# Up projections by Strassen's scheme in an attention kernel with two feed-forward layers

## The chip, the core and the metric

The kernel runs on one core of one Trainium2 chip. The metric is the device time of one execution in microseconds (us). The engines are TensorE (PE for its matmuls, PEld for its weight loads), VectorE (DVE), ScalarE (ACT), GpSimd (POOL) and SyncE (SP), which here issues nearly all DMAs.

## The reference

```python
B, H, S, D = 4, 8, 576, 64           # masked softmax attention, 32-wide local or strided masks
attn = softmax(mask(q @ k.T / sqrt(D))) @ v
x = attn.transpose(0, 2, 1, 3).reshape(2304, 512)
h = x @ w_in                          # 512 -> 2048
x = (h * tanh(log(1 + exp(h)))) @ w_out            # 2048 -> 512
h = maximum(maximum(x @ w1, x @ w2), x @ w3)       # three up projections, 512 -> 768
out = h @ w_out2                      # down projection, 768 -> 512
```

Inputs are drawn at random; the weights come to the chip as 8-byte floats and are taken apart there.

## The kernel before

Every fp32 product is made of three matmuls: each operand is kept as a high and a low part (fp32r), and `PASSES` names the pairs high·high, high·low, low·high. So one 128-feature by 512-token block with its four slices of 128 input channels takes 12 matmuls. Tokens lie in five blocks, four of 512 and one of 256.

The stages overlap only at their ends. Attention; then `raw`, the first four of sixteen feature blocks of `w_in`; then their part of `w_out` into x2, stored to DRAM (`x2p`); then the other twelve feature blocks (`into_h`, L516, and x2 matmuls L543, called the h stage here), block of tokens by block of tokens, with the stored part added (`whole`, L563 to L570) and x2 split into high and low parts; then the last layer, called the up stage here: for each block of tokens and each of six feature blocks three up projections (`up`, L590) into a ring of four PSUM banks, the maximum of the three (`m1` on ACT, L596; `m2` on DVE, L599), its split into the high and low halves of `g` (L601, L602), and the down projection (`down`, L615) into `acc0` to `acc3`.

A weight block of 128 x 512 is loaded (L787, L790) into a slot, turned into fp32 by one ACT operation (L253) and three DVE operations (L257, L261, L267), and split by one of ACT (L277) and one of DVE (L281). There are 24 slots. The weights of the last layer are converted while the h stage ends, in its last block of 256 tokens.

The order on each engine is not that of the code: `build_plan` adds every step with its engine, estimated cost, and what it reads and writes to a `Plan`; the plan simulates the engines, gives each step a due time by running backward, repeats this, and writes out the best order. The engines work through their lists in that fixed order, and wait for each other by semaphores. Where the plan sees PE idle before the first x2 matmul, it puts matmuls on zeros (`fill`).

Of the kernel before, what the change touches and what calls it, by code (L numbers as in the profile page):

```python
# [10 lines left out]
F32 = mybir.dt.float32  # L11
F32R = mybir.dt.float32r
# [15 lines left out]
SLOTS_Y = 8  # L28
W_EXP = 8
EB = 96  # L30
REST = 5376
# [158 lines left out]
def build_plan(k, B, H, S, D, DM, FF, FF2, wide):  # L190
# [33 lines left out]
    for f in range(F1, FC):  # L224
        for kind in ("in", "out"):
            order.append((kind, f))
            need[kind, f] = n_a1 + f - F1
    for f in range(F2C):
        for j, kind in enumerate(("1", "2", "3", "out2")):
            order.append((kind, f))  # L230
            need[kind, f] = n_a + 1.5 * f + 0.3 * j
    slot_of = {}
    free_slots = [("a", i) for i in range(SLOTS_A)]

    def load_and_convert(key):
# [8 lines left out]
        extra = {"x": [("attn",)], "y": [("hrdone",)]}.get(slot[0], [])  # L244
# [5 lines left out]
        add("w_load", "sp", nbytes / 360, load, reads=extra, writes=[hk, lk] if wide else [wk], rank=rank - 3)  # L250
        if wide:
# [23 lines left out]

        def hi():
            nc.scalar.copy(out=k.open_slot(slot)[:, 0, :], in_=k.wt(r2).bitcast(F32))  # L277

        def lo():
            s = k.slot(slot)  # L280
            nc.vector.tensor_tensor(out=s[:, 1, :], in0=k.wt(r2).bitcast(F32), in1=s[:, 0, :], op=ALU.subtract)  # L281

        add("w_hi", "act", act(512), hi, reads=[wk], writes=[hk], rank=rank)
        add("w_lo", "dve", dve(512), lo, reads=[wk, hk], writes=[lk], rank=rank)
# [263 lines left out]

    def part(s, bi):
        t0, n = blocks[bi]  # L550
        for c in range(KC):
            e = ring("ev")
            add("ev", "act", act(n, psum=True), (lambda c=c, e=e: nc.scalar.mul(k.work("ev", e)[:, :n], k.bank(f"acc{c}")[:, :n], W_SCALE)),
                reads=[("bank", f"acc{c}")], writes=[("ev", e)], rank=s)
            add("x2p_st", "sp", P * n * 4 / 360, (lambda c=c, e=e: nc.sync.dma_start(out=k.x2p[:, c, t0:t0 + n], in_=k.work("ev", e)[:, :n])),
                reads=[("ev", e)], writes=[("x2p", bi, c)], rank=s)

    def whole(s, bi):
# [19 lines left out]
    def up(bi, f, rank):
        rm, rg = ring("h"), ring("g")
        MK, G0, G1 = ("h", rm), ("g", rg, 0), ("g", rg, 1)  # L580
        t0, n = blocks[bi]
        m_ = lambda: k.work("h", rm)[:, :n]
        g = lambda: k.g(rg)
        for w_ in ("1", "2", "3"):
            hb = hring[hcount[0] % len(hring)]
            hcount[0] += 1
            for c in range(KC):
                def h_mm(c=c, hb=hb, w_=w_):
                    for m, (a, q) in enumerate(PASSES):
                        nc.tensor.matmul(  # L590
                            k.bank(hb)[:, :n], lhsT=wap((w_, f), a, c), rhs=k.x[:, q, c, t0:t0 + n],
                            start=(c == 0 and m == 0), stop=(c == KC - 1 and m == 2),
                        )
                add("u_mm", "pe", 3 * mm(n), h_mm, reads=wkeys((w_, f)) + [("x2", bi, c)], writes=[("bank", hb)], rank=rank)
            if w_ == "1":
                add("m1", "act", act(n, psum=True), (lambda hb=hb: nc.scalar.copy(out=m_(), in_=k.bank(hb)[:, :n])),  # L596
                    reads=[("bank", hb)], writes=[MK], rank=rank)
            else:
                add("m2", "dve", dve(n), (lambda hb=hb: nc.vector.tensor_tensor(out=m_(), in0=k.bank(hb)[:, :n], in1=m_(), op=ALU.max)),  # L599
                    reads=[("bank", hb)], writes=[MK], rank=rank)  # L600
# [6 lines left out]
    def down(bi, f, rg, rank):  # L607
        t0, n = blocks[bi]
        key = ("out2", f)
        for c in range(n // P):  # L610
            ab = f"acc{c}"
# [8 lines left out]
            if f == F2C - 1:  # L620
                o_ = ring("wt")
                o = lambda o_=o_: k.wt(o_).bitcast(F32)
                if c % 2:
                    add("o", "dve", dve(DM), (lambda ab=ab, o=o: nc.vector.tensor_scalar(
                        out=o(), in0=k.bank(ab)[:], scalar1=W_SCALE, scalar2=None, op0=ALU.mult)),
                        reads=[("bank", ab)], writes=[("wt", o_)], rank=rank)
                else:
                    add("o", "act", act(DM, psum=True), (lambda ab=ab, o=o: nc.scalar.mul(o(), k.bank(ab)[:], W_SCALE)),
                        reads=[("bank", ab)], writes=[("wt", o_)], rank=rank)
                add("o_st", "sp", P * DM * 4 / 360, (lambda c=c, o=o: nc.sync.dma_start(  # L630
                    out=k.out[t0 + c * P:t0 + (c + 1) * P, :], in_=o())), reads=[("wt", o_)], rank=rank)
# [5 lines left out]
    free_slots.extend(("x", i) for i in range(SLOTS_X))  # L637
    s = 0
    for bi in range(NB1):
        for f in range(F1):  # L640
            raw(s, bi, f, RAW_BANKS[s % len(RAW_BANKS)])
            s += 1
    for f in range(F1):
        release(("in", f))
# [8 lines left out]
    add("ypool", "dve", 0, k.open_ypool, writes=[("hrdone",)], rank=s - 1)  # L653
    free_slots.extend(("y", i) for i in range(SLOTS_Y))
# [4 lines left out]
    for bi, (t0, n) in enumerate(blocks):  # L659
        for c in range(KC):  # L660
            e = ring("ev")
            xp_ring[bi, c] = e
            add("x2p_ld", "sp", P * n * 4 / 360, (lambda c=c, e=e, t0=t0, n=n: nc.sync.dma_start(
# [227 lines left out]
```

## Time and profile before

| what | value |
|---|---|
| median of 3 runs | 801.85 us (801.34 to 802.04) |
| profiled execution: span from first to last instruction | 801.2 us |
| PE matmul busy | 793.7 us, 99% of the span |
| DVE busy | 361.0 us, 45% |
| ACT busy | 321.1 us, 40% |

The page gives no other time for the profiled execution than its span; the three timed runs lie 0.1 to 0.8 us above it, which is what lies around a span. A PE that reads 99% busy has nearly no gap in front of a matmul; how long one matmul keeps PE is read from the starts of matmuls that follow each other, since the busy time of each overlaps the next.

### The profile page before, as it was taken

The numbers are of one execution on the slowest core, as the hardware profiler recorded it, in microseconds if no ns is written. First come the engines' busy times: TensorE is split into PE (matmuls) and PEld (weight loads), VectorE is DVE, ScalarE is ACT, GpSimd is POOL, SyncE is SP. The second block draws the span as 40 slices with busy tenths as digits, with TensorE's granted clock in tenths as the row PEclk, the third lists the DMA queues.
The fourth block names the chain that finished last, engine by engine and source line by source line (L and its number), as shares of the span: only waits on it lengthen the run. The fifth ranks groups of instructions, "written<-read, shape, count | busy, mean of one in ns | idle before, by whom it ended". The sixth has DMA issues, their size and how long they took to land.

```text
span 801.2 us, 12605 instructions
## 1 busy us (share of the span) xinstructions
PE 793.7 (99%) x5017; PEld 670.4 (84%) x5017; DVE 361.0 (45%) x769; ACT 321.1 (40%) x839; POOL 4.4 (1%) x22
## 2 busy tenths in 40 slices
PE   9999999999999999999999999999999999999998
PEld 7878888988888888888888889888888888888897
DVE  6998886895941311311221169981222221122222
ACT  5988878996731322321322257631110111110111
POOL 2000000000000000000000000000000000000000
PEclk9999999999999999999999999999999999999999
DMA  9787750944900100100010069300100010010010
GB/s 212 156 158 125 134 105 22 351 149 163 334 2 1 53 0 1 54 0 1 1 53 0 1 224 325 109 1 0 53 1 0 13 41 1 0 53 1 0 53 27
DMA packets 119690, 59.66 MB, mean 74 GB/s; under 512 B 91984, under 2 KB 110416, under 8 KB 119632
## 3 DMA queue, kind: packets, MB, share of 16 engines
q1 hardware_dynamic: 118448, 58.57, 26.2%
q8 instruction: 39, 0.64, 0.3%
q10 hardware_dynamic: 1184, 0.30, 0.2%
q14 instruction: 19, 0.16, 0.1%
HBM read 49.41 MB, written 9.44 MB: 73 GB/s over the span
## 4 chain that ended last, share of the span: by engine, by line
PE 88%; DMA 4%; SPq 3%; DVE 3%; ACT 1%; issue 1%; DVEq 0%; ACTq 0%
PE bank_acc L543 23%; PE bank_a L590 21%; PE bank_a L516 12%; PE bank_acc L615 9%; PE bank_h L516 7%; PE bank_h L590 7%; PE bank_acc L516 3%; DMA wslot<-in_moe_w_dram 1%; DMA v<-in_v_dram 1%; PE bank_a L413 1%; PE bank_a L471 1%; SPq L809 1%; PE bank_a L458 1%; PE bank_acc L413 1%; PE bank_acc L471 1%; DMA wslot<-in_moe_w_out_dram 1%
## 5 line engine op out<-in xcount | busy, mean ns | idle before, releaser
L543 PE MATMUL bank_acc<-g,wslot 128*128 128x512 f32 (+1 forms) x960 | 205.1, 369 | 1.5 <-DVE g L538 0.7
L543 PEld LDWEIGHTS bank_acc<-g,wslot 128*128 128x128 f32 x960 | 168.3, 188 | 33.6 <-DVE g L538 2.0
L590 PE MATMUL bank_a<-x,wslot 128*128 128x512 f32 (+1 forms) x816 | 173.2, 367 | 0.0
L590 PEld LDWEIGHTS bank_a<-x,wslot 128*128 128x128 f32 x816 | 142.4, 189 | 25.5
L538 DVE TENSOR_TENSOR g<-h,g 128x512 fp32r<-128x512 f32 (+1 forms) x80 | 50.9, 636 | 192.1 <-ACT g L537 192.0
L516 PE MATMUL bank_a<-x,wslot 128*128 128x512 f32 (+1 forms) x540 | 116.2, 368 | 0.0
L516 PEld LDWEIGHTS bank_a<-x,wslot 128*128 128x128 f32 x540 | 94.6, 189 | 16.8
L599 DVE TENSOR_TENSOR h<-bank_a,h 128x512 f32<-128x512 f32 (+1 forms) x46 | 29.1, 633 | 137.3 <-PE bank_a L590 137.3
L615 PE MATMUL bank_acc<-wslot,g 128*128 128x512 f32 x324 | 78.3, 389 | 0.0
L516 PE MATMUL bank_h<-x,wslot 128*128 128x288 f32 (+2 forms) x372 | 74.2, 338 | 0.0
L615 PEld LDWEIGHTS bank_acc<-wslot,g 128*128 128x128 f32 x324 | 60.4, 188 | 12.3
L535 ACT ACTIVATE h<-bank_a 128x512 f32<-128x512 f32 (+1 forms) x45 | 25.0, 554 | 108.8 <-PE bank_a L516 108.8
L516 PEld LDWEIGHTS bank_h<-x,wslot 128*128 128x128 f32 x372 | 58.5, 188 | 7.1
L601 ACT ACTIVATE g<-h 128x512 fp32r<-128x512 f32 (+1 forms) x30 | 17.6, 588 | 114.9 <-DVE h L599 114.9
L590 PE MATMUL bank_h<-x,wslot 128*128 128x512 f32 (+1 forms) x264 | 58.3, 370 | 0.0
L438 ACT ACTIVATE s<-s,st 118x54 f32<-118x54 f32 (+1 forms) x160 | 55.2, 348 | 7.0 <-DVE st L432 6.7
L590 PEld LDWEIGHTS bank_h<-x,wslot 128*128 128x128 f32 x264 | 46.7, 188 | 8.6
L537 ACT CAST g<-h 128x512 fp32r<-128x512 f32 (+1 forms) x80 | 46.1, 577 | 4.4 <-PE bank_acc L543 2.6
L253 ACT ACTIVATE wt<-wslot 128x512 f32<-128x512 f32 x56 | 37.9, 678 | 21.6 <-DVE wslot L281 9.6
L277 ACT CAST wslot<-wt 128x512 fp32r<-128x512 f32 x56 | 34.3, 620 | 14.7 <-DVE wt L267 14.3
L596 ACT COPY h<-bank_a 128x512 f32<-128x512 f32 (+1 forms) x22 | 12.0, 547 | 69.0 <-PE bank_a L590 69.0
L281 DVE TENSOR_TENSOR wslot<-wt,wslot 128x512 fp32r<-128x512 f32 x56 | 38.2, 684 | 2.6 <-ACT wslot L277 2.5
(71 smaller groups left out, 680.2 us busy)
## 6 DMA issues: line engine op xcount, KB each, us to landing
wslot<-in_moe_w_out_dram SPq DMA_DIRECT2D x22, 512.0 KB
wslot<-in_moe_w_dram SPq DMA_DIRECT2D x18, 512.0 KB
wslot<-in_moe_w_in_dram SPq DMA_DIRECT2D x16, 512.0 KB
out_dram<-wt SPq DMA_DIRECT2D x18, 256.0 KB
x2p<-ev SPq DMA_DIRECT2D x16, 256.0 KB
ev<-x2p SPq DMA_DIRECT2D x16, 256.0 KB
rawq<-in_q_dram SPq DMA_DIRECT2D x48, 72.0 KB
rawk<-in_k_dram SPq DMA_DIRECT2D x48, 72.0 KB
```

The costliest lines, as they stand in the source:

```text
L253: nc.scalar.mul(k.wt(r2).bitcast(F32), k.words(slot)[1].bitcast(F32), 2.0 ** -111)
L277: nc.scalar.copy(out=k.open_slot(slot)[:, 0, :], in_=k.wt(r2).bitcast(F32))
L281: nc.vector.tensor_tensor(out=s[:, 1, :], in0=k.wt(r2).bitcast(F32), in1=s[:, 0, :], op=ALU.subtract)
L438: nc.scalar.activation(sv()[:, j, :], sv()[:, j, :], AF.Exp, bias=mx()[:, j:j + 1], accum_out=dn()[:, j:j + 1],)
L516: nc.tensor.matmul(k.bank(hb)[:, :n], lhsT=wap(("in", f), a, c), rhs=k.x[:, q, c, t0:t0 + n], start=(c == 0 and m == 0), stop=(c == KC - 1 ...
L535: add(name, "act", act(n, psum=not stored), lambda: nc.scalar.activation(Hh(), src(), AF.Mish, scale=W_SCALE), reads=sread, writes=[HK], r ...
L537: add("gh", "act", act(n), lambda: nc.scalar.copy(out=g()[:, 0, :n], in_=Hh()), reads=[HK], writes=[G0], rank=s)
L538: add("gl", "dve", dve(n), lambda: nc.vector.tensor_tensor(out=g()[:, 1, :n], in0=Hh(), in1=g()[:, 0, :n], op=ALU.subtract), reads=[HK, G0 ...
L543: nc.tensor.matmul(k.bank(f"acc{c}")[:, :n], lhsT=wap(("out", f), a, c), rhs=g()[:, q, :n], start=(first and m == 0), stop=(last and m == 2),)
L590: nc.tensor.matmul(k.bank(hb)[:, :n], lhsT=wap((w_, f), a, c), rhs=k.x[:, q, c, t0:t0 + n], start=(c == 0 and m == 0), stop=(c == KC - 1 a ...
L599: add("m2", "dve", dve(n), (lambda hb=hb: nc.vector.tensor_tensor(out=m_(), in0=k.bank(hb)[:, :n], in1=m_(), op=ALU.max)), reads=[("bank", ...
L615: nc.tensor.matmul(k.bank(ab)[:], lhsT=k.g(rg)[:, a, c * P:(c + 1) * P], rhs=t[:, q, :], start=(f == 0 and m == 0), stop=(f == F2C - 1 and ...
```

## The change

The three up projections are taken out of `up`. Features go in pairs of 128-blocks, tokens in pairs of 384 (`SP`), so x2 falls into three "pairs" of tokens. With the left operand (two feature blocks by two halves of the 512 channels: A11, A12, A21, A22) and the right operand (two halves of the channels by two halves of the tokens: B11 to B22), each 256 x 768 output is formed by Winograd's form of Strassen's scheme: seven products of half blocks (`product`, L722), six matmuls of 384 columns each, where eight would be needed. The outer loop runs over nine sets (three pairs of feature blocks times `w1`, `w2`, `w3`), the inner one over the three pairs of tokens: 27 units.

- Sums of weights S1 to S4 are made when a set's two weights are converted (`set_convert`, four DVE additions of 256 columns), and then split like weights.
- Differences of tokens T1, T2, T3 and N21 are made once per pair (`pair_operands`): 20 DVE operations and 8 low halves on DVE, 8 high halves on ACT, all of 384 columns. N21 takes the place of B12 in `x`. Those of pairs 0 and 1 come in the h stage; pair 2 ends with the last block of tokens, so its own come after it.
- The sums of products are formed in three PSUM banks per unit (two sets of banks take turns). Bank `Bk` is the narrow one: ACT copies the first product into it, three products accumulate onto it, and between these ACT copies it out (`copy(Bk, u2)`) and DVE reads it (`result(Bk, m22, p7)`). A unit with `w1` has two DVE operations and five ACT copies; one with `w2` or `w3` has six DVE operations and three ACT copies.
- The maxima live in the tiles `g`, `h` and `ev`, go to DRAM (`h2`) after the third weight, and come back for the down projection, which is now a stage of its own after all up projections (`h2_ld`, split, `down`), with two sets of four banks in turn.
- There are 16 slots for 24. The twelve feature blocks of the h stage are done in two sweeps of six over all tokens, with the partial x2 stored and loaded once more.

```diff
-SLOTS_Y = 8
+SWEEP = 6
+SP = 384
+T_SLOTS = (5, 6, 7, 8, 9, 10)
+CP_SLOT = 4
...
+    sweeps = [range(f, f + SWEEP) for f in range(F1, FC, SWEEP)]
...
+    def pair_operands(s, p):
...
+            steps = [(lambda: o(a, 0), bt, ALU.subtract, opkeys(p, a, j) + b_key), (t, lambda: o(a, 1), ALU.add, opkeys(p, a, j))]
+            if not b_f32:
+                steps.append((t, lambda: o(b, 1), ALU.subtract, opkeys(p, b, j)))
...
+        for j in range(2):
+            home.clear()
+            difference("T1", "B12", "B11", j)
+            difference("T3", "B22", "B12", j)
+            split("T3", j)
+            difference("T2", "B22", "T1", j)
+            split("T1", j)
+            difference("N21", "B21", "T2", j)
+            split("T2", j)
+            split("N21", j)
...
+    def set_convert(i, rank):
...
+        for out, a, b, op in (
+            ((s12, 0), (w2_, 0), (w2_, 1), ALU.add), ((s12, 1), (s12, 0), (w1_, 0), ALU.subtract),
+            ((s34, 0), (w1_, 0), (w2_, 0), ALU.subtract), ((s34, 1), (w1_, 1), (s12, 1), ALU.subtract),
+        ):
...
+    def strassen(i, w_, f, p, rank):
...
+        A, D, Bk = (("a0", "a2", "acc0"), ("a1", "h0", "acc1"))[u % 2]
+        p7, u2 = ("cp", u % 2), ("h", 2)
...
+                for j in range(2):
+                    for (pa, pb) in PASSES:
+                        nc.tensor.matmul(
+                            k.bank(bank)[:, :SP], lhsT=left(i, a, pa, j), rhs=operand(p, "B12" if b == "N21" else b, pb, j),
+                            start=start and n == 0, stop=n == 5, skip_group_check=True,
+                        )
...
+        product(A, "A11", "B11", True)
+        copy(A, ("bank", Bk))
+        product(D, "S3", "T3", True)
+        copy(D, p7)
+        product(A, "A12", "B21", False)
+        result(A, m11)
+        product(Bk, "S2", "T2", False)
+        copy(Bk, u2)
+        product(D, "A22", "N21", False)
+        result(D, m21, u2)
+        product(Bk, "S1", "T1", False)
+        result(Bk, m22, p7)
+        product(Bk, "S4", "B22", False)
+        result(Bk, m12)
+        if w_ == "3":
...
+                add("h2_st", "sp", P * SP * 4 / 360, (lambda m=m, ff=ff, t0=t0: nc.sync.dma_start(
+                    out=k.h2[:, ff, t0:t0 + SP], in_=home(m))), reads=[m], writes=[("h2", ff, t0 // SP)], rank=rank)
...
     def up(bi, f, rank):
...
-        for w_ in ("1", "2", "3"):
-            hb = hring[hcount[0] % len(hring)]
...
-                add("u_mm", "pe", 3 * mm(n), h_mm, reads=wkeys((w_, f)) + [("x2", bi, c)], writes=[("bank", hb)], rank=rank)
...
+        add("h2_ld", "sp", P * n * 4 / 360, lambda: nc.sync.dma_start(out=m_(), in_=k.h2[:, f, t0:t0 + n]),
+            reads=[("h2", f, b) for b in range(NT // SP) if b * SP < t0 + n and (b + 1) * SP > t0], writes=[MK], rank=rank - 3)
...
+    for w, sweep in enumerate(sweeps):
+        final = w == len(sweeps) - 1
+        for bi, (t0, n) in enumerate(blocks):
+            part_load(w, s, bi)
+            for f in sweep:
...
+            add_part(w, s - 1, bi, final)
...
+            while final and 2 * SP * (pairs_done + 1) <= t0 + n:
+                pair_operands(s, pairs_done)
+                pairs_done += 1
+    u = 0
+    for i, (w_, f) in enumerate(sets):
+        for p in range(n_pairs):
+            strassen(i, w_, f, p, s_end + span * u)
+            u += 1
...
     for bi in range(NB):
         for f in range(F2C):
-            rank = s + 2.0 * (bi * F2C + f)
+            rank = s + 0.5 * (bi * F2C + f)
             ent = up(bi, f, rank)
-            down(*ent, rank + 3)
+            down(*ent, rank + 1)
```

PE in the middle of the last layer, before: in `bank_a0` to `bank_h0` the up projections of one block, in `bank_acc0` to `bank_acc3` the down projection; `x` holds x2.

```order
L590 MATMUL bank_a2_103<-x_66,wslot_4786 128x512 x12
L590 MATMUL bank_h0_104<-x_66,wslot_4806 128x512 x12
L615 MATMUL bank_acc0_105<-wslot_4827,g1_81 128x512 x3
L615 MATMUL bank_acc1_106<-wslot_4827,g1_81 128x512 x3
L615 MATMUL bank_acc2_107<-wslot_4827,g1_81 128x512 x3
L615 MATMUL bank_acc3_108<-wslot_4827,g1_81 128x512 x3
L590 MATMUL bank_a0_101<-x_66,wslot_4844 128x512 x12
L590 MATMUL bank_a1_102<-x_66,wslot_4868 128x512 x12
L590 MATMUL bank_a2_103<-x_66,wslot_4889 128x512 x12
```

PE now, in a unit of the fifth set (`w2`); `ty` holds the T operands of pairs 0 and 1, and bank `acc0` is this unit's `Bk`; a semaphore that the instruction waits for stands in brackets.

```order
L722 MATMUL bank_acc0_110<-ty_2738,wslot_5439 128x384 x6
L722 MATMUL bank_a2_108<-x_66,wslot_5427 128x384 [waits Activation_49]
L722 MATMUL bank_a2_108<-x_66,wslot_5427 128x384 x5
L722 MATMUL bank_acc0_110<-ty_2738,wslot_5439 128x384 [waits Activation_49]
L722 MATMUL bank_acc0_110<-ty_2738,wslot_5439 128x384 x5
L722 MATMUL bank_a1_107<-x_66,wslot_5305 128x384 x6
L722 MATMUL bank_acc0_110<-x_66,wslot_5449 128x384 [waits DVE_49]
L722 MATMUL bank_acc0_110<-x_66,wslot_5449 128x384 x5
L722 MATMUL bank_h0_109<-ty_2738,wslot_5449 128x384 x6
L722 MATMUL bank_acc1_111<-ty_2738,wslot_5439 128x384 [waits Activation_49]
```

Twelve matmuls into one bank became six; the second and third accumulation into `acc0` each wait for ACT or DVE, with one product of another bank in front of them.

DVE in the same stage before: the maxima (L599) and the low half of `g` (L602).

```order
L599 TENSOR_TENSOR h0_73<-bank_h0_104,h0_73 128x512
L599 TENSOR_TENSOR h0_73<-bank_a0_101,h0_73 128x512
L602 SCALAR_TENSOR_TENSOR g0_80<-h0_73,g0_80 128x512
L599 TENSOR_TENSOR h1_74<-bank_a2_103,h1_74 128x512
L599 TENSOR_TENSOR h1_74<-bank_h0_104,h1_74 128x512
L602 SCALAR_TENSOR_TENSOR g1_81<-h1_74,g1_81 128x512
L599 TENSOR_TENSOR h2_75<-bank_a1_102,h2_75 128x512
L599 TENSOR_TENSOR h2_75<-bank_a2_103,h2_75 128x512
```

DVE now, at the start of the Strassen stage: operands of pair 2 (L630 differences in `wt`, L641 low halves) with the first results (L745) among them.

```order
L630 TENSOR_TENSOR wt1_70<-x_66 128x384
L641 TENSOR_TENSOR wslot_4839<-wt2_71,wslot_4839 128x384
L630 TENSOR_TENSOR wt1_70<-wt1_70,x_66 128x384
L630 TENSOR_TENSOR wt0_69<-wt0_69,x_66 128x384
L630 TENSOR_TENSOR wt1_70<-wt1_70,x_66 128x384
L630 TENSOR_TENSOR wt3_72<-wt3_72,x_66 128x384
L630 TENSOR_TENSOR wt0_69<-wt0_69,x_66 128x384
L745 TENSOR_TENSOR g_4833<-bank_a2_108,h2_75 128x384
L641 TENSOR_TENSOR wslot_4842<-wt1_70,wslot_4842 128x384
L641 TENSOR_TENSOR x_66<-wt3_72,x_66 128x384
L630 TENSOR_TENSOR wt2_71<-x_66,wt0_69 128x384
L745 TENSOR_TENSOR g_4834<-bank_acc0_110,wslot_4836 128x384
```

Between two reads that hand a PSUM bank back to PE there now stand operations on SBUF alone, and later in the stage those of the conversion of weights (L264 to L292, L681).

## Rows read from the trace of the kernel before

**Rows 1.** the page: busy time by engine, and the granted clock in 40 slices.
```profile
PE 793.7 (99%) x5017; PEld 670.4 (84%) x5017; DVE 361.0 (45%) x769; ACT 321.1 (40%) x839; POOL 4.4 (1%) x22
...
PEclk9999999999999999999999999999999999999999
```

**Rows 2.** windows by stage: busy us of PE, PEld, DVE, ACT, POOL; clock, DMA.
```profile
160.00:180.00 20.00, 20.00 (x89) 16.55 (x89) 20.00 (x37) 19.36 (x37) 0.00 (x0) 1.00 0.42 153
204.00:464.59 260.59, 260.36 (x1147) 215.03 (x1147) 70.98 (x114) 78.56 (x133) 0.00 (x0) 1.00 0.10 34
464.59:502.61 38.02, 36.88 (x292) 35.53 (x291) 33.15 (x67) 25.41 (x53) 0.00 (x0) 1.00 0.93 307
502.61:797.24 294.63, 294.63 (x1403) 248.12 (x1401) 91.14 (x155) 53.60 (x95) 0.00 (x0) 1.00 0.06 20
```

**Rows 3.** the page: groups of the up and down projections, and a weight load.
```profile
L590 PE MATMUL bank_a<-x,wslot 128*128 128x512 f32 (+1 forms) x816 | 173.2, 367 | 0.0
...
L615 PE MATMUL bank_acc<-wslot,g 128*128 128x512 f32 x324 | 78.3, 389 | 0.0
...
L590 PE MATMUL bank_h<-x,wslot 128*128 128x512 f32 (+1 forms) x264 | 58.3, 370 | 0.0
...
L590 PEld LDWEIGHTS bank_a<-x,wslot 128*128 128x128 f32 x816 | 142.4, 189 | 25.5
```

**Rows 4.** the chain that ended last: start, us, engine, tile, line, count.
```profile
741.48 2.72 PE bank_h L590 x12
...
774.72 1.44 PE bank_h L590 x12
```

**Rows 5.** timeline, PE, matmuls of 288 columns: start, us, engine, line, operation, count.
```profile
148.21 1.76 PE L516 MATMUL bank_acc<-x,wslot 128*128 128x288 f32 x12
149.81 1.76 PE L516 MATMUL bank_h<-x,wslot 128*128 128x288 f32 x12
```

**Rows 6.** groups by line and shape: DVE reading PSUM, 512 and 256 columns.
```profile
L599 DVE TENSOR_TENSOR h<-bank_a,h 128x512 f32<-128x512 f32 x36 | 24.9, 690 | 118.4 <-PE bank_a L590 118.4
...
L599 DVE TENSOR_TENSOR h<-bank_a,h 128x256 f32<-128x256 f32 x10 | 4.3, 425 | 18.9 <-PE bank_a L590 18.9
```

**Rows 7.** the same for ACT.
```profile
L596 ACT COPY h<-bank_a 128x512 f32<-128x512 f32 x18 | 10.5, 586 | 60.2 <-PE bank_a L590 60.2
...
L596 ACT COPY h<-bank_a 128x256 f32<-128x256 f32 x4 | 1.5, 372 | 8.9 <-PE bank_a L590 8.9
```

**Rows 8.** timeline, DVE without idle time: operations that follow each other.
```profile
502.26 1.41 DVE L563 SCALAR_TENSOR_TENSOR ev<-bank_acc,ev 128x256 f32<-128x256 f32 x4
...
506.33 0.68 DVE L261 SCALAR_TENSOR_TENSOR wt<-wslot,wt 128x512 uint32<-128x512 uint32 x1
...
506.93 0.42 DVE L257 TENSOR_SCALAR wt<-wt 128x512 uint32<-128x512 uint32 x1
...
507.27 0.68 DVE L281 TENSOR_TENSOR wslot<-wt,wslot 128x512 fp32r<-128x512 f32 x1
```

**Rows 9.** timeline, hand-over between PE and DVE or ACT.
```profile
484.91 0.43 DVE L538 TENSOR_TENSOR g<-h,g 128x256 fp32r<-128x256 f32 x1
...
485.39 0.77 PEld L543 LDWEIGHTS bank_acc<-g,wslot 128*128 128x128 f32 x6 [0.28 <-DVE g L538]
...
512.84 0.61 PE L590 MATMUL bank_a<-x,wslot 128*128 128x512 f32 x2
...
513.04 0.59 ACT L596 COPY h<-bank_h 128x512 f32<-128x512 f32 x1 [0.49 <-PE bank_h L590]
...
572.68 2.88 PE L615 MATMUL bank_acc<-wslot,g 128*128 128x512 f32 x12
572.88 0.69 DVE L599 TENSOR_TENSOR h<-bank_a,h 128x512 f32<-128x512 f32 x1 [1.96 <-PE bank_a L590]
```

**Rows 10.** timeline, PE in the change of stages, with idle time and its releaser.
```profile
475.79 3.02 PE L543 MATMUL bank_acc<-g,wslot 128*128 128x256 f32 x23 [0.49 <-DVE g L538]
```

**Rows 11.** timeline, the last two stores.
```profile
797.41 1.11 SPq L630 DMA_DIRECT2D out_dram<-wt  x2
```

More of the change, by code (lines that the diff above doesn't have):

```diff
@@ L223, in build_plan @@
         need["in", f], need["out", f] = f, n_raw + f
[L224 to L231, printed above, removed]
+    for i, sweep in enumerate(sweeps):
+        for f in sweep:
+            for kind in ("in", "out"):
+                order.append((kind, f))
+                need[kind, f] = n_a1 + i * NB * SWEEP + f - sweep[0]
     slot_of = {}
-    free_slots = [("a", i) for i in range(SLOTS_A)]
+    free_slots = list(range(SLOTS_A))
     def load_and_convert(key):
@@ L565, in whole @@
                 op0=ALU.mult, op1=ALU.add)), reads=[("bank", ab)], writes=[("ev", e)], rank=s)
-        for c in range(KC):
+            if not last:
+                store_part(i + 1, s, bi, c, e)
+        for c in range(KC) if last else ():
             e = xp_ring[bi, c]
             add("x2_hi", "act", act(n), (lambda c=c, e=e: nc.scalar.copy(out=k.x[:, 0, c, t0:t0 + n], in_=k.work("ev", e)[:, :n])),
-                reads=[("ev", e)], writes=[("x2", bi, c)], rank=s + 0.5)
+                reads=[("ev", e)], writes=[("x2", bi, c, 0)], rank=s + 0.5)
@@ new lines, in build_plan, with set_slots, set_load @@
+    set_of = {}
+    def set_slots(n):
+        got = [x for x in free_slots if x not in RESERVED][:n]
+        for x in got:
+            free_slots.remove(x)
+        return got
+    def set_load(i, w_, f, rank):
+        slot, = set_slots(1)
+        n = len(set_of.setdefault(i, []))
+        set_of[i].append(slot)
+        add("w_load", "sp", P * 4096 / 360, lambda: k.load_weight(w_, f + n, k.stage(slot)),
+            reads=[("attn",)], writes=[("slot", slot, 0), ("slot", slot, 1)], rank=rank)
@@ L578, in up @@
     def up(bi, f, rank):
-        rm, rg = ring("h"), ring("g")
-        MK, G0, G1 = ("h", rm), ("g", rg, 0), ("g", rg, 1)
+        rm, rg = ring("wt"), ring("g")
+        MK, G0, G1 = ("wt", rm), ("g", rg, 0), ("g", rg, 1)
         t0, n = blocks[bi]
-        m_ = lambda: k.work("h", rm)[:, :n]
+        m_ = lambda: k.wt(rm)[:, :n].bitcast(F32)
         g = lambda: k.g(rg)
-        for w_ in ("1", "2", "3"):
-            hb = hring[hcount[0] % len(hring)]
[L586 to L593, printed above, removed]
-                add("u_mm", "pe", 3 * mm(n), h_mm, reads=wkeys((w_, f)) + [("x2", bi, c)], writes=[("bank", hb)], rank=rank)
[L595 to L600, printed above, removed]
@@ L642, in build_plan @@
             s += 1
+    convert_ready()
     for f in range(F1):
@@ new lines, in build_plan, with advance @@
+    n_pairs = NT // (2 * SP)
+    n_set = [0, 0]
+    span = 1.35
+    def advance(s0):
+        room = lambda: len([x for x in free_slots if x not in RESERVED])
+        while True:
+            i, c = n_set[0] // 2, n_set[1]
+            if c < n_set[0] // 2 and room() >= 2:
+                set_convert(c, s0 + span * n_pairs * c - 4)
+                n_set[1] += 1
+            elif i < len(sets) and i <= c and room() >= 1:
+                set_load(i, *sets[i], s0 + span * n_pairs * i - 8)
+                n_set[0] += 1
+            else:
+                return
@@ new lines, in build_plan @@
+    u = 0
[3 more added lines that the diff above has]
+            u += 1
+        free_slots.extend(set_of[i])
+        advance(s_end)
+        if n_set[1] == len(sets):
+            order.extend(("out2", f_) for f_ in range(F2C) if ("out2", f_) not in need)
+            for f_ in range(F2C):
+                need["out2", f_] = s_end + span * len(sets) * n_pairs + f_ * 0.5
+            usable = [x for x in free_slots if x not in RESERVED]
+            free_slots[:] = usable
+            convert_ready()
```

214 lines of the change are left out of this document (168 added, 46 removed), and 3 rows, old and new, of the table M_HOME.

## The prediction

> **What bounds the kernel now.** I read the page first: PE is busy 793.7 of 801.2 us, and its clock stands at full speed (2.4 GHz) in all 40 slices [rows 1]. The reader is to see that no other engine can be the bound on average, and that only fewer or shorter matmuls can bring much. Then the windows by stage [rows 2]. The last layer, 502.61 to 797.24, has PE busy without a gap and DVE at 91.14 of 294.63 us, 31%. The h stage, 204 to 464.59, is much the same. Between them lie 38.02 us in which weights of the last layer are converted while PE runs the block of 256 tokens, with DVE at 33.15, 87%.
>
> Third, what one matmul costs, from starts in the chain and the timeline. Twelve matmuls of 512 columns take 2.72 us, 226.7 ns each, and twelve of 256 take 1.44, 120 ns [rows 4]. At 2.4 GHz the columns alone are 213.3 and 106.7 ns, so both leave 13.3 ns. Twelve of 288 columns take 149.81 - 148.21 = 1.60 us, 133.3 ns, again 120 + 13.3 [rows 5]. A matmul of 384 columns is then 160 + 13.3 = 173.3 ns. This is the number on which all rests; no row shows it, but rows on both sides do.
>
> **Up projections.** Before there are 816 + 264 = 1080 of them [rows 3]: 18 blocks of features and weights, each with 48 of 512 and 12 of 256 columns, so 864 x 0.2267 + 216 x 0.120 = 221.8 us. With the 324 of the down projection at 0.2267 (73.4 us) this is 295.2, and the stage lasts 294.63 with three of them done before it: it holds nothing but matmuls. Now there are 27 units of seven products of six matmuls, 1134 x 0.1733 = 196.6 us. Saved: 25.2 us. Two extra matmuls that open banks `acc0` and `acc1` (L752) give back 0.35. A unit is 7.28 us, a product 1.04.
>
> One rule speaks against smaller matmuls. The trace has a weight load at 189 ns on the mean, longer than the 173 of a matmul [rows 3], yet twelve matmuls with twelve loads pass in 1.44 us: loads lie behind matmuls. The Trainium skill (TensorE: Matmul & The Clock Gate, "The mechanism" in Part 3) says that a weight load overlaps a running matmul only where their row groups differ, and here all use the whole array; with its 107 ns for 128 columns ("LDWEIGHTS (loading the stationary operand)") the saving would be (864 x 0.320 + 216 x 0.214) - 1134 x 0.267 = 20 us, as an estimate from these pages. The 13.3 ns left of 120 speak against it.
>
> **The change of stages.** From 464.59 to 502.61 PE has 12 x 24 = 288 matmuls of 256 columns and three of 512 to do, 35.24 us, and takes 38.02: 2.8 us are lost, such as the 0.49 in which x2 waits for a low half behind conversions on DVE [rows 2, 10]. That stretch goes. In its place the first sweep's last block of 256 tokens has the conversions of eight weights and the first set beside it, with DVE about as full, but for half as long: I take 1.5 us (0 to 2.8). The second storing and loading of partial x2 goes through SP, which has nothing else in the h stage, and its four additions per block on DVE lie beside 32.6 us of matmuls; nothing.
>
> **Operands of pair 2.** They can begin only after the last block, and units 0 and 1 with the first product of unit 2 (some 13 us in PE's list) run before PE needs the first of them. DVE operations follow each other at (1.41 - 0.41) / 3 = 0.33 us with 256 columns and 0.60 with 512 [rows 8]; halfway, 0.47, for 384. 28 of these are 13.2 us; eight of 256 columns for x2 go before, 2.7, less the 1.1 us by which the first bank is ready early. PE needs T3 of both channel slices first, 21 operations in: about 12 us. It just fits; I take 0.5 us (0 to 5, if ACT's halves hold DVE up).
>
> **Hand-backs.** This is what the trace before does not have. In each unit ACT must read `Bk` before S1 x T1 adds to it, and DVE before S4 x B22; in PE's list one product, 1.04 us, stands in front of each. ACT and DVE begin 0.20 us after the product ends, and PE's weight load follows 0.05 after they end [rows 9]. A DVE read of 384 columns is halfway between 425 and 690 ns, 0.56; an ACT copy between 372 and 586, 0.48 [rows 6, 7]. So 0.81 and 0.73 of 1.04 us are used: a margin of 0.23 and 0.31, if the engine is free. It need not be. DVE has 126 result operations (9 units with two, 18 with six) x 0.47 = 59 us, seven sets to convert at 2 x (0.34 + 2 x 0.60) + 4 x 0.33 + 3 x 0.60 + 0.33 = 6.6, so 46, six weights of the down projection at 2.14, 13, and pair 2's 13: 131 of 197 us, 67%. An operation of 0.60 that has just begun spends the margin; behind the late read stand all later ones of DVE's list, and PE waits for these too. Bounds: from 160 to 180 us DVE is busy 20.00 of 20.00 and PE loses nothing; in the change of stages at 87% PE loses 2.78 of 38.02, 7.3%, which would be 14.4 of 197 us [rows 2]. I take 3 us, nearer to the lower end, 0.06 us for each of 54 hand-backs: the load is lower than in both, and the plan has put conversions where it expects a gap.
>
> **Down projection alone.** Its 73.4 us stay. Per block and feature block PE needs 2.72 us; ACT's 0.6 and DVE's 0.6 fit. What was in SBUF now comes from DRAM. The last two stores show the price: issued from 797.41 on, both landed by the end of the span at 801.2, under 3.8 us each [rows 11]. A store and a load are then at most 7.6 us, but only pair 2's data are young, and they are used after three blocks, 49 us later; four `wt` buffers cover loads at 2.72 us a step. What can be late is the first `g`, whose buffers still hold results of pair 1 until stored: one unit of cover, 7.28 us. I take 0.5 us (0 to 2). The end is as before: the last bank, a copy, a store.
>
> **Sum.** 801.2 - 25.2 + 0.35 - 2.8 + 1.5 + 0.5 + 3 + 0.5 = 779.05 us of span. The median of the runs is 0.65 above the span of the profiled execution, so 779.7 us.
>
> **Rivals.**
> - Hand-backs cost at the rate of the change of stages: 14.4 in place of 3 gives 791. For it speaks that lists in fixed order lost just so with DVE at 87%; against it DVE's 67%, and that set 0 and 1 are converted before. Chance 0.2 (784.5 to 797).
> - Slower than before: every hand-back finds a conversion of 0.60 and a maximum of 0.47 in front of it, so is late by 1.07 - 0.25 = 0.8 us; 54 of these are 44, and the time is 821. It decides from 0.46 us on the mean, where 54 x 0.46 eats 25. For it: DVE's maxima follow directly on its reads (L745, L748 in its list). Against: PE's list alternates two units, so it has other banks to work on. Chance 0.06.
> - The change doesn't do what it says: matmuls of 384 columns run at the pace of their weight loads, 189 ns [rows 3]. 1134 x 0.189 = 214.3, a saving of 7.5: 797. Against it stand the 120 ns of 256 columns. The skill's rule above would give some 785, and by that row it falls with this rival. Chance 0.05.
> - Nothing is lost anywhere: 801.2 - 25.2 + 0.35 - 2.8 = 773.6 of span, 774.2. Part of my own range, chance of below it 0.04.
>
> **Numbers.** My forecast has 0.65, from 774.2 to 784.5. The range takes in most of the first rival: 774 to 792. Faster by over 0.2% (about what a measurement of this kernel can tell from no change), below 800.2: 0.65 + 0.2 + 0.05 + 0.04 less a little for 797 being near: 0.92. Within 0.2%: 0.02. Slower: 0.06.
>
> **What would show it.** In the changed profile: products of L722 start 1.04 us after each other where nothing waits (else the pace of 384 columns is wrong); the Strassen stage lasts about 200 us with the idle time before its matmuls released by DVE and ACT and 3 us in sum (over 10: the first rival); the first use of T3 of pair 2 waits under 1 us; the down stage has PE without a gap from its second block on; DVE stands at about two thirds in the Strassen stage. Wrong would be the forecast if PE's idle time there is spread over all units at more than 0.2 us a hand-back, or if the clock falls from 2.4 to 1.2 GHz anywhere behind a wait.

## The result, and the profile after

The changed kernel takes 775.96 us (median; 775.44 to 776.39), the kernel before 801.6: a ratio of 0.9675 (95%: 0.9661 to 0.969), 3.3% faster. The forecast was 779.7 us with a range of 774 to 792. The profiled execution has a span of 773.7 us, 27.5 less than before; the medians lie 25.6 apart, and the entry on the time around the span, further below, says why.

The page of the changed kernel: busy time by engine, and the granted clock in 40 slices.

```profile
PE 766.2 (99%) x5073; PEld 677.9 (88%) x5073; DVE 464.8 (60%) x993; ACT 368.3 (48%) x950; POOL 4.4 (1%) x22
...
PEclk9999999999999999999999999999999999999999
```

PE is still the bound, and less of it is needed than in [rows 1]. The granted clock reads 9 (90% or more of 2.4 GHz) in all slices, and 1.00 in the windows below. DVE has 104 us more work. Windows by stage (busy us of PE, PEld, DVE, ACT, POOL; clock, DMA): two stretches of the h stage, its end, the products, the down projection.

```profile
342.50:346.20 3.70, 3.58 (x27) 3.33 (x28) 3.70 (x9) 2.96 (x6) 0.00 (x0) 1.00 1.06 369
346.20:360.00 13.80, 13.80 (x82) 12.23 (x81) 13.80 (x29) 9.69 (x19) 0.00 (x0) 1.00 0.81 268
...
460.90:498.89 37.99, 37.99 (x238) 34.37 (x237) 26.23 (x53) 17.37 (x37) 0.00 (x0) 1.00 0.18 56
...
498.89:697.50 198.61, 198.61 (x1145) 198.09 (x1144) 142.91 (x282) 81.39 (x166) 0.00 (x0) 1.00 0.28 90
697.50:769.60 72.10, 72.10 (x319) 59.51 (x318) 24.26 (x39) 21.19 (x37) 0.00 (x0) 1.00 0.47 150
```

In the last three PE has no idle time at all, though DVE stands at 142.91 of 198.61 us, 72%, in the stage of products; before, the last layer had it at 31% [rows 2]. The 38 us ahead of the last layer hold 37.99 us of PE work in 37.99, where 1.14 were idle before [rows 2]. The only wait of PE behind 201.45 us that the list of waits shows is in the middle of the h stage, where the second sweep's weights are converted and DVE is full:

```profile
342.50 3.61 PE L554 MATMUL bank_acc<-g,wslot 128*128 128x256 f32 x24 [0.75 <-ACT g L548]
```

This wait differs from execution to execution: the profile of the changed kernel's second run below doesn't have it, the other runs have 0 to 0.68 us there, and the first run of the eight plain products has 1.57.

Where the 27.5 us came from, by the starts of the stages on PE's timeline (last layer means up and down projections):

| | before | after | difference |
|---|---|---|---|
| to the start of the sweeps | 202.67 | 201.45 | -1.22 |
| sweeps (three matmuls of the last layer, 0.68 us, taken off before) | 299.26 | 297.44 | -1.82 |
| last layer, to PE's end | 295.31 | 270.73 | -24.58 |
| tail | 3.96 | 4.08 | +0.12 |

The first line is no work of the change: TensorE's instructions stand there in the same order, and in the other runs below with that order the sweeps begin between 201.06 and 203.54 us.

One hand-back of each kind in the timeline (start, us, engine, line, operation; product S1 x T1 begins at 548.15, S4 x B22 at 550.23):

```profile
547.11 1.20 PE L722 MATMUL bank_a<-x,wslot 128*128 128x384 f32 x6
...
547.30 0.48 ACT L732 COPY h<-bank_acc 128x384 f32<-128x384 f32 x1
...
548.15 1.20 PE L722 MATMUL bank_acc<-ty,wslot 128*128 128x384 f32 x6
...
548.94 0.55 DVE L745 TENSOR_TENSOR h<-bank_a,h 128x384 f32<-128x384 f32 x1
549.19 1.20 PE L722 MATMUL bank_a<-x,wslot 128*128 128x384 f32 x6
549.41 0.55 DVE L745 TENSOR_TENSOR wslot<-bank_acc,wslot 128x384 f32<-128x384 f32 x1
549.88 0.55 DVE L748 TENSOR_TENSOR g<-h,g 128x384 f32<-128x384 f32 x1
550.23 1.03 PE L722 MATMUL bank_acc<-x,wslot 128*128 128x384 f32 x5
```

Products start 1.04 us apart. The copy ends at 547.78, 0.37 us before S1 x T1; the read ends at 549.96, 0.27 before S4 x B22, although another read (548.94) stands right before it. Over all 27 units the DVE read ends at least 0.19 us ahead (19 of 27 between 0.19 and 0.29), the ACT copy at least 0.09 (most 0.36). Behind the copy with 0.09 a product starts 0.06 us late; no other hand-back was late.

### The profile page after: what moved, and what is told of

It reads as the page before. It is cut to its first block, busy times and chain, and to the rows that moved or that the text cites. A ratio compares the mean times of both kernels' runs of the same rounds, so it can differ in the third digit from the quotient of the medians.

```text
span 773.7 us, 13318 instructions
## 1 busy us (share of the span) xinstructions
PE 766.2 (99%) x5073; PEld 677.9 (88%) x5073; DVE 464.8 (60%) x993; ACT 368.3 (48%) x950; POOL 4.4 (1%) x22
## 4 chain that ended last, share of the span: by engine, by line
PE 91%; SPq 4%; DMA 2%; DVE 1%; ACT 1%; issue 1%; DVEq 0%
PE bank_acc L554 25%; PE bank_a L527 14%; PE bank_a L722 11%; PE bank_acc L722 11%; PE bank_h L527 8%; PE bank_acc L797 5%; PE bank_h L722 3%; PE bank_acc L527 3%; PE bank_a L797 3%; DMA wslot<-in_moe_w_in_dram 1%; PE bank_a L424 1%; PE bank_a L482 1%; SPq L1046 1%; PE bank_h L797 1%; PE bank_a L469 1%; PE bank_acc L482 1%
## 5 line engine op out<-in xcount | busy, mean ns | idle before, releaser
L527 PE MATMUL bank_a<-x,wslot 128*128 128x512 f32 (+1 forms) x540 | 116.0, 368 | 0.0
L527 PEld LDWEIGHTS bank_a<-x,wslot 128*128 128x128 f32 x540 | 94.6, 189 | 16.9
L722 PE MATMUL bank_a<-x,wslot 128*128 128x384 f32 x408 | 80.9, 334 | 0.0
L722 PEld LDWEIGHTS bank_a<-x,wslot 128*128 128x128 f32 x408 | 71.6, 188 | 0.0
L527 PEld LDWEIGHTS bank_h<-x,wslot 128*128 128x128 f32 x372 | 58.6, 188 | 7.2
L288 ACT CAST wslot<-wt 128x512 fp32r<-128x512 f32 (+1 forms) x74 | 43.8, 596 | 24.9 <-DVE wt L274 21.1
L260 ACT ACTIVATE wt<-wslot 128x512 f32<-128x512 f32 x56 | 37.8, 681 | 33.4 <-DMA wslot<-in_moe_w_dram 16.9
L292 DVE TENSOR_TENSOR wslot<-wt,wslot 128x512 fp32r<-128x512 f32 (+1 forms) x74 | 47.6, 654 | 7.4 <-ACT wslot L288 7.3
L797 PE MATMUL bank_acc<-wslot,g 128*128 128x512 f32 x180 | 44.6, 389 | 0.0
L722 PE MATMUL bank_acc<-ty,wslot 128*128 128x384 f32 x216 | 43.3, 334 | 0.0
L268 DVE SCALAR_TENSOR_TENSOR wt<-wslot,wt 128x512 uint32<-128x512 uint32 x56 | 38.4, 687 | 0.8
L274 DVE SCALAR_TENSOR_TENSOR wt<-wslot,wt 128x512 uint32<-128x512 uint32 x56 | 38.1, 685 | 0.5
L722 PEld LDWEIGHTS bank_acc<-ty,wslot 128*128 128x128 f32 x216 | 37.9, 188 | 0.1
```

Source lines behind the costliest of these rows:

```text
L260: nc.scalar.mul(k.wt(r2).bitcast(F32), k.words(slot)[1].bitcast(F32), 2.0 ** -111)
L268: nc.vector.scalar_tensor_tensor(out=t, in0=k.words(slot)[1], scalar=0x80000000, in1=t, op0=ALU.bitwise_and, op1=ALU.bitwise_or)
L274: nc.vector.scalar_tensor_tensor(out=t, in0=k.words(slot)[0], scalar=29, in1=t, op0=ALU.logical_shift_right, op1=ALU.bitwise_or)
L288: nc.scalar.copy(out=k.open_slot(slot)[:, 0, :n], in_=k.wt(r2)[:, c0:].bitcast(F32))
L292: nc.vector.tensor_tensor(out=s[:, 1, :n], in0=k.wt(r2)[:, c0:].bitcast(F32), in1=s[:, 0, :n], op=ALU.subtract)
L527: nc.tensor.matmul(k.bank(hb)[:, :n], lhsT=wap(("in", f), a, c), rhs=k.x[:, q, c, t0:t0 + n], start=(c == 0 and m == 0), stop=(c == KC - 1 ...
```

## The experiments

Theory: the gain is matmul columns, and the hand-backs are free because the planner's lists put each read at the head of its engine's queue when its product ends, so the 0.2 to 0.3 us of margin is never used up. Rivals: the new stage order itself gains; or a loss grows with DVE's load and was only small here by luck. Since the starts of the sweeps differ from run to run by a microsecond or two, I compare the last layer's stretch (270.73 us in the changed kernel) beside the times.

**The changed kernel again.** 

> The changed kernel once more, unaltered, beside the others on the same chip: 775 to 777.5 us, and no stop of the stream of products in its stage.

775.52 us, ratio 0.9668 (0.9654 to 0.9683); last layer again 270.73 us.

**Eight plain products.** All that belongs to the seven-product scheme is out: S, T, the hand-backs.

```diff
-        product(A, "A11", "B11", True)
...
-        result(Bk, m12)
+        for n_, (m, r, c) in enumerate(((m11, 1, 1), (m21, 2, 1), (m12, 1, 2), (m22, 2, 2))):
+            bank = six[(4 * u + n_) % 6]
+            product(bank, f"A{r}1", f"B1{c}", True)
+            product(bank, f"A{r}2", f"B2{c}", False)
+            result(bank, m)
```

> The changed kernel with the eight plain half-block products in place of the seven of the scheme: same pairs, same columns of 384, same stage order, same bounce of the up layer through DRAM; the S and T operands, their splits and the hand-backs are left out since nothing reads them, the result is unchanged. Theory A (the gain is matmul columns and nothing else): 27 units x 6 x 8 x 173.3 ns = 224.6 us for 196.6, less 0.35 us for the two opening matmuls: 775.96 + 27.7 = 803.7 us (802.7 to 804.7), so 2 us slower than the kernel before although its stage order is the new one. Theory B (the new stage order alone brings a good part, say the 2.8 us of the old change of stages and more): under 801 us. Theory C (S, T and the hand-backs cost something in the changed kernel that the trace hides): the difference to 775.96 is clearly under 27 us.

> The eight plain products in the new stage order as before, with the fourth block of weights now read where it lies (in the first run of this kind the products of A22 read A21's words). Theory A (columns and nothing else): 27.7 us above the changed kernel, 803.7 us (802.5 to 804.7), above the kernel before. Theory B (the new stage order alone gains): under 801 us.

804.48 us the first time (A22's products then read A21's words), 804.10 with the right block, ratio to before 1.0026 (1.0015 to 1.0037). Theory A holds: seven products for eight are worth 28.6 us beside the changed kernel on the same chip (27.7 expected), and pairs outermost with columns of 384 and a down stage of its own cost some 2 us by themselves. No part of the gain is the stage order's.

**DVE's hand-back read doubled**, in unchanged order.

```diff
-  add("s_m", "dve", dve(SP), lambda: nc.vector.tensor_tensor(out=home(to), in0=b(), in1=home(other), op=ALU.add),
+  add("s_m", "dve", dve(SP), lambda: (other == p7 and nc.vector.tensor_scalar(out=b(), in0=b(), scalar1=1.0, scalar2=None, op0=ALU.mult), nc.vector.tensor_tensor(...)),
```

> Every engine's order is the changed kernel's, but VectorE works on the S1 x T1 bank twice before it hands it back to S4 x B22: an in-place multiplication by 1 first, then the addition. In the changed kernel's trace 20 of the 27 hand-backs of this kind end 0.19 to 0.28 us before S4 x B22 starts, and a second VectorE instruction of 384 columns adds 0.47 us (their spacing back to back). Theory A (the hand-backs are free only because one product in front, 1.04 us, is longer than read and hand-over): 20 starts late by about 0.23 to 0.27 us each, together 4.6 to 5.4 us: 781 us (780 to 783), with gaps of some 0.25 us ahead of S4 x B22 in the trace. Theory B (a late hand-back drags the VectorE queue along, as my slower rival had it): 0.8 us and more for each of 54, over 800 us. Theory C (the product waits for nothing that VectorE does there): 776 us.

786.54 us, ratio 0.9807 (0.9782 to 0.9832); last layer +10.55 us. The mechanism is theory A's, the size twice what I expected. The timeline of that kernel:

```profile
543.96 1.21 PE L722 MATMUL bank_a<-x,wslot 128*128 128x384 f32 x6
...
544.26 0.56 DVE L745 TENSOR_SCALAR bank_acc<-bank_acc 128x384 f32<-128x384 f32 x1
544.85 0.56 DVE L745 TENSOR_TENSOR wslot<-bank_acc,wslot 128x384 f32<-128x384 f32 x1
...
545.46 1.31 PE L722 MATMUL bank_acc<-x,wslot 128*128 128x384 f32 x6 [0.30 <-DVE wslot L745]
546.61 1.20 PE L722 MATMUL bank_a<-ty,wslot 128*128 128x384 f32 x6
```

The second instruction needs the first one's result and follows after 0.59 us, not 0.47. S4 x B22 starts 1.50 us after the product before it, so 0.46 late, of which the profile shows 0.30 as idle: it still counts the last matmul of the product before, 1.20 - 1.04 = 0.16 us, as busy. The product behind starts 1.15 us later, another 0.11. Twenty hand-backs are late in this way, nineteen by 0.48 to 0.59 us in all and one by 0.38: 10.4 of the 10.55.

**The same, with its length told to the planner** (`(2 if other == p7 else 1) * dve(SP)` as the cost).

> The same doubled VectorE work, but the planner is given its length, so it may order the products anew. Theory A (the planner's order is what hides the hand-backs): it puts a second product in front of S4 x B22, whose margin is then about 0.8 us: 776.5 us (775.5 to 778). Theory B (there is no second product to put there, the banks are all taken): as the doubled read in the old order, 780 to 783 us.

780.86 us, ratio 0.9739 (0.9703 to 0.9774): outside the interval I gave for A, but its last layer is +3.27 for +10.55. Two thirds of the loss go by order alone. Theory A's mechanism is there: two products or more now stand in front of S4 x B22 in nearly all units, where it was one in most, and the read mostly ends 0.6 to 0.7 us ahead. What is left in the last layer is mainly three waits of 2.5 us together, two of them near its end; the rest of the time lies in the sweeps (298.23 us) and in front, which the planner ordered anew too.

**ACT's copy doubled**, in unchanged order.

```diff
-  add("s_cp", "act", act(SP, psum=True), lambda: nc.scalar.copy(out=dst(), in_=k.bank(bank)[:, :SP]),
+  add("s_cp", "act", act(SP, psum=True), lambda: [nc.scalar.copy(out=dst(), in_=k.bank(bank)[:, :SP]) for _ in range(2 if to == u2 else 1)],
```

> TensorE's and VectorE's orders are the changed kernel's; ScalarE does the copy of the S2 x T2 bank twice (27 times) before it hands the bank back to S1 x T1. In the changed kernel's trace the copy ends 0.36 us before S1 x T1 starts in most units, hand-over 0.05 us; a second copy adds 0.38 us (their spacing back to back) to 0.5 us, so some 22 products start late by 0.07 to 0.2 us. Theory A (what a late hand-back costs is its lateness): 1.5 to 4.4 us, 777.5 to 780.5 us. Theory B (each stop of the stream of products also costs a fixed 0.28 us, as the kernel with the doubled VectorE read showed: 0.21 to 0.30 us of wait, but the products 0.50 to 0.60 us late): 22 x (0.07 to 0.2 + 0.28) = 7.7 to 10.6 us, 784 to 786.5 us.

782.58 us, ratio 0.9759 (0.9745 to 0.9774), last layer +6.48: between the two theories, and the rows say that neither is right.

```profile
548.91 1.21 PE L722 MATMUL bank_a<-x,wslot 128*128 128x384 f32 x6
550.15 1.31 PE L722 MATMUL bank_acc<-ty,wslot 128*128 128x384 f32 x6
551.30 1.21 PE L722 MATMUL bank_a<-x,wslot 128*128 128x384 f32 x6
```

```profile
549.11 0.99 ACT L732 COPY h<-bank_acc 128x384 f32<-128x384 f32 x2
```

The copies end at 550.10 and PE goes on 0.05 later: 1.24 us after the last start, 0.20 late with no idle time shown, and 0.11 more on the product behind. So a late hand-back costs its lateness and 0.11 to 0.13 us; the 0.28 of my theory B was 0.16 of lateness hidden in a modelled end and 0.12 of restart. Nineteen products are late, not 22: seventeen by 0.20 us and two by 0.36 and 0.40, with the restarts 6.3 of the 6.48 us.

**One set of banks for all units.**

```diff
-        A, D, Bk = (("a0", "a2", "acc0"), ("a1", "h0", "acc1"))[u % 2]
+        A, D, Bk = ("a0", "a2", "acc0")
...
-        if u < 2:
+        if u < 1:
```

> All 27 units use one set of three banks in place of two sets in turn, the planner orders the products for that. Theory A (a product of another bank of the same or the next unit is enough cover, 1.04 us against 0.7 to 0.8 us of hand-back): each bank's chain in one unit, for the third bank copy 0.5, three products of 1.04, two hand-backs of 0.7 to 0.8 and one read of 0.8, is 5.9 us and so shorter than the unit's 7.28 us: 777 us (776 to 780). Theory B (the second set of banks is what makes the hand-backs free): two hand-backs of 0.7 to 0.8 us stand bare in each of 27 units, 38 to 43 us: about 815 us; with one bare, about 796 us.

785.86 us, ratio 0.9802 (0.9777 to 0.9827); last layer +8.34 us. Neither: the planner finds cover for most hand-backs (B fell), but not for all. PE's longest waits in the stage are for the copy into `Bk`:

```profile
PE bank_acc L722 <- ACT bank_acc L732: 1.9, 5, 0.5
```

Five such waits, one of 0.23 for DVE and eight slips of 0.2 to 0.3 us without one shown come with their restarts to 6.7 of the 8.34 us; smaller slips make the rest.

**More DVE work that hands nothing back**, in unchanged order: one or three more maxima behind the last result of 18 units.

```diff
-  add("s_m", "dve", dve(SP), lambda: nc.vector.tensor_tensor(out=home(m), in0=b(), in1=home(m), op=ALU.max),
+  add("s_m", "dve", dve(SP), lambda: [nc.vector.tensor_tensor(out=home(m), in0=home(m) if j_ else b(), in1=home(m), op=ALU.max) for j_ in range(4 if m == m12 else 1)],
```

> TensorE's and ScalarE's orders are the changed kernel's; VectorE does one more 384-column max (of the result with itself) behind the last result of each of the 18 units of the second and third matrix, which hands nothing back: VectorE's load in the stage of products goes from 72% to about 77%. Theory A (loss comes only when a delayed VectorE instruction overruns the 0.2 us margin of a hand-back; VectorE's idle pieces take up the rest): the changed kernel's VectorE rows moved on by 0.59 us each time overrun it 4 times, by 1.1 us together, and with 0.28 us for each stop 2.2 us: 778 us (776.5 to 779). Theory B (the loss goes with VectorE's load, as the prediction's 3 us at 67%): 779.5 us and more.

> As the kernel with one more VectorE instruction in 18 units, but three: VectorE's load about 88%. Theory A: 12 hand-backs overrun their margin by 12.5 us together at most (each stop of TensorE gives VectorE time, so less in the end, 6 to 12.5), and 12 stops at 0.28 us add 3.4 us: 785 to 792 us. Theory B (VectorE is not the bound below full load, the delays vanish in its idle 28%): 776 to 778 us. Theory C (the slower rival of the prediction, every hand-back 0.8 us late once VectorE queues): 810 us and more.

With one: 778.83 us, ratio 0.9714 (0.9698 to 0.973), last layer +3.15; just inside the interval of theory A. With three: 795.58 us, ratio 0.9924 (0.9906 to 0.9941), +18.83; above what I gave A, below C. I had counted DVE's late reads alone, but most of the waits are for ACT: two of three with one more maximum, ten of twelve with three. The timeline with three (DVE, ACT and PE):

```profile
555.54 1.74 DVE L741 TENSOR_TENSOR g<-g 128x384 f32<-128x384 f32 x3
557.20 0.68 DVE L274 SCALAR_TENSOR_TENSOR wt<-wslot,wt 128x512 uint32<-128x512 uint32 x1
```

```profile
557.98 0.62 ACT L288 CAST wslot<-wt 128x512 fp32r<-128x512 f32 x1 [2.00 <-DVE wt L274]
558.50 0.47 ACT L732 COPY h<-bank_acc 128x384 f32<-128x384 f32 x1
```

```profile
556.34 1.21 PE L722 MATMUL bank_a<-x,wslot 128*128 128x384 f32 x6
559.02 1.33 PE L722 MATMUL bank_acc<-ty,wslot 128*128 128x384 f32 x6 [1.48 <-ACT h L732]
```

ACT stands at a weight's high half (L288) until DVE has done L274 behind the three maxima; the copy that PE needs is queued behind L288, its product done before. The waits for that copy are 11.8 us in 10 places, those for DVE's own reads 2.3. In all ten places a weight operation (L288, once L260) is what ACT does right before the copy.

**The three maxima, with their length told to the planner.**

> The three more VectorE instructions in each of 18 units, with their length given to the planner. With the orders unaltered they cost 18.8 us in the stages of products and down projection, because ScalarE waits for a weight conversion on VectorE with a hand-back queued behind it. Theory A (what decides is the order in the queues, not VectorE's load of 88%): the planner orders the conversions and the products anew and at least two thirds go, as with the doubled read told (10.6 to 3.3 us): 778 to 783 us. Theory B (at this load no order helps): 790 us and more.

777.72 us, ratio 0.9696 (0.9675 to 0.9718): 2.2 us above the changed kernel on the same chip, last layer +1.75. Its window of the stage of products:

```profile
498.90:697.50 198.60, 198.40 (x1147) 197.61 (x1146) 164.99 (x328) 81.41 (x165) 0.00 (x0) 1.00 0.26 85
```

DVE is at 83% (I had worked out 88), and PE is idle for 0.2 us; with late starts that show no wait, the products lose 0.8 us. The other 1.2 or so are at the start of the down stage, where PE waits for the first `g`:

```profile
707.30 1.93 PE L797 MATMUL bank_acc<-wslot,g 128*128 128x512 f32 x6 [0.65 <-ACT g L783]
```

The same work in the old order lost 18.83 us; DVE was then busy for 170.2 of 216.9 us of the stage, 78%. So at these loads, 83% at most, the order in the queues decides what is lost, and the load does not; what a still fuller DVE costs in this stage was not tried.

**Pair 2 first.** `for p in (2, 0, 1)` within each set.

> The three pairs of token halves in the order 2, 0, 1 within each set of weights; pair 2 is the one whose T operands are made after the last sweep, in the changed kernel from 500.4 us on, with its first T product at 511.7 us. Theory A (the pairs in front are the cover; taken away, TensorE waits for T): eight to sixteen VectorE instructions at 0.47 us stand in front of the first T product, and only two products without T of this pair can fill: 3 to 6 us, 779 to 782 us. Theory B (the planner takes products of pairs 0 and 1 out of turn whatever the order says): 776 to 777 us.

792.13 us, ratio 0.9882 (0.9858 to 0.9906), last layer +15.54: theory A's mechanism, larger than expected, and a second wait that I had not named.

```profile
504.05 0.91 PE L722 MATMUL bank_a<-wslot 128*128 128x384 f32 x3
510.98 0.69 PE L722 MATMUL bank_a<-wslot 128*128 128x384 f32 x1 [6.03 <-ACT wslot L639]
512.31 1.01 PE L722 MATMUL bank_a<-wslot 128*128 128x384 f32 x2 [0.64 <-DVE wslot L641]
```

```profile
708.81 0.73 PE L797 MATMUL bank_acc<-wslot,g 128*128 128x512 f32 x2 [2.56 <-ACT g L783]
710.06 2.01 PE L797 MATMUL bank_acc<-wslot,g 128*128 128x512 f32 x4 [0.52 <-DVE g L784]
```

PE waits 6.67 us for T3, and then for the first `g` of the down stage, since pair 0's last results now come one unit later. The list of waits has 10.4 us in all. Some 3.2 of the other 5 are the clock's. Windows of that kernel (clock is the number behind POOL's):

```profile
490.00:504.50 14.50, 14.50 (x106) 14.22 (x105) 13.72 (x32) 8.93 (x20) 0.00 (x0) 1.00 0.12 40
504.50:510.90 6.40, 0.45 (x2) 0.14 (x2) 6.40 (x15) 2.49 (x5) 0.00 (x0) 0.83 0.00 0
510.90:513.10 2.20, 1.48 (x3) 1.08 (x4) 2.20 (x5) 0.83 (x3) 0.00 (x0) 0.50 0.00 0
513.10:515.60 2.50, 2.50 (x9) 2.50 (x9) 1.90 (x4) 0.86 (x3) 0.00 (x0) 0.50 0.00 0
515.60:517.70 2.10, 2.06 (x11) 1.74 (x11) 0.69 (x1) 0.90 (x2) 0.00 (x0) 1.00 0.00 0
...
708.80:714.00 5.20, 4.68 (x12) 3.46 (x13) 3.61 (x6) 1.62 (x3) 0.00 (x0) 0.67 0.46 139
```

A window's clock is its mean. In 6.4 us with PE busy for 0.45 the granted clock falls to 0.50, that is 1.2 GHz (at 508.8), and from 515.6 on it is 1.00 (2.4 GHz) again; behind the second wait it is 0.50 from 710.2 to 713.6. By the starts, eleven matmuls of 384 columns take up to 0.32 us each for 0.17 in the first stretch, and eight of 512 columns 0.43 for 0.23 in the second: 1.6 us each time. Most of the rest is what each of the five stops costs beside the wait that is shown, 0.16 + 0.11 us. In no other run of this study did PE stand so long in these stages, and the clock of the changed kernel's stages is 1.00 in every window shown.

## Why the prediction was right, and where its sum was off

- **The pace of 384 columns: right.** Products of six start 1.04 us apart, 173 ns a matmul. A weight load takes 188 ns on the mean there:

```profile
L722 PEld LDWEIGHTS bank_a<-x,wslot 128*128 128x128 f32 x408 | 71.6, 188 | 0.0
```

  PEld is busy 198.09 of 198.61 us beside a PE that is never idle, so loads overlap matmuls here on the whole array, and the rival by which loads set the pace (189 ns, 797 us) is out. The 20 us that followed from the Trainium skill (TensorE: Matmul & The Clock Gate, "The mechanism" in Part 3) go with it. Its list there allows the overlap only where row groups differ, but the text above the list also lets a load into the background weight buffer run ahead, which the prediction left out. This case agrees with the second; that such a buffer was used, no run shows.
- **Up projections -25.2 + 0.35: right.** Seven products, the two opening matmuls and the down projection are 196.56 + 0.35 + 73.45 = 270.36 us of matmuls; the stretch lasts 270.73.
- **Hand-backs +3: the step that failed.** The durations (0.55 and 0.48 for 0.56 and 0.48) and the margins (0.2 to 0.3 and 0.36 for 0.23 and 0.31) were about right, the DVE load was 72% for 67; the loss was 0.06 us for 3. I took it from a load, between two stretches of other stages; what decides is whether an instruction that something waits on stands behind another in its queue. The rival of 791 us, read from the loss at 87%, fell for the same reason: 17.5 us with DVE full (342.5 to 360) lose PE 0.75 us here, and 83% with lists made for it lose 0.8 us in all the products.
- **The change of stages -2.8 + 1.5:** measured -1.82 for -1.3; the new loss is that one wait of 0.75 us, which the second run of the changed kernel doesn't have.
- **Pair 2's operands +0.5:** nil, and "it just fits" was right. The last low half of T3 ends at 510.66, its first product starts at 511.72:

```profile
510.11 0.55 DVE L641 TENSOR_TENSOR wslot<-wt,wslot 128x384 fp32r<-128x384 f32 x1
```

  With the cover gone, PE waited 6.67 us, above my bound of 5, and lost 1.6 more to the clock, as I had named among what would make the forecast wrong.
- **Down stage's start +0.5:** nil; with pair 0 done one unit later there are waits of 2.56 and 0.52 us, above the bound of 2.
- **Slower rival (821):** such late hand-backs are real, as the run with three maxima shows (+18.83 of the 44), but only where work comes in that the lists do not know of. Both costs that the planner was told of came down by two thirds or more.
- **The time around the span:** 0.65 us was taken for what lies around a span, and that was wrong. In every execution on record for which both are given, of either kernel, the time is 1.73 to 1.86 us above the span of the same execution. The profiled execution before, with its span of 801.2, thus took about 803 us, longer than the three timed ones, and the profiled one after, 775.44, is the shortest of its four. The error did no harm: the forecast stands, by this difference, on their median of 801.85. But it is why the two spans differ by 27.5 us and the medians by 25.6; the 1.22 us at the start, which nothing of the change explains, are part of that.

The terms of loss came to 5.5 us, and 0.75 + 0.37 were found (the 0.37 is the last layer beside its 270.36 us of matmuls). By the right terms the forecast would have been 801.85 - 25.2 + 0.35 - 2.8 + 0.75 + 0.37 = 775.3 us; measured were 775.96. "Nothing is lost anywhere", to which I gave 0.04 below its time, was the nearest of the cases; I had it in my own range, but put the value in the middle of the bounds where the lower bound was the better guess.

## What to carry to other kernels

Where instruction lists are fixed ahead, price a new hand-over by its own chain (end of the product, start of the reader, end, next start) against the work in front of it, and ask for each in-order queue what stands ahead of the instruction that is waited for; the engine's mean load does not tell. Where the chains fitted (here by 0.2 us in nearly all units) and the orders were made with durations close to the measured ones (469 ns for a DVE operation of 384 columns in the kernel's cost function, 0.47 us measured), the loss was as good as nil; one kernel shows this. Work that the lists are not told of can cost TensorE a good part of its length though it hands nothing back, by way of a second queue: 54 more maxima, 0.59 us each, lost 18.83 us.

## What the runs showed of the hardware

- A late hand-back costs PE its lateness and 0.11 to 0.13 us on the product behind; the idle time that the profile shows is 0.16 us short of the lateness, as the last matmul's modelled end covers it, so a stop of 0.20 us shows as none (the runs with the doubled read and the doubled copy).
- A DVE instruction on 384 columns that needs the result of the one before follows after 0.59 us, one that doesn't after 0.47.
- With pair 2 first, the granted clock is 0.50 from 508.8 to 515.6 us, where PE is idle from 505 to 511, and from 710.2 to 713.6, behind a wait of 2.56 us. Waits of up to 2.01 us in the run with three maxima leave it at 1.00 (all windows from 495 to 780 us), but in the first run of the eight plain products a wait of 1.57 us that ends at 345.7 is followed by 0.50 from 347.5 to 350.9.
- DVE can be full for 13.80 of 13.80 us (346.20 to 360.00) with PE busy for all of them.
